# A power-of-two scale's sum over partitions takes its PSUM buffer from another pool, in an attention and hard-swish kernel

## The chip, the cores and the metric

The kernel runs on one core of a Trainium2 chip. The metric is the device time in microseconds (us), as the median of several runs. The engines are named as in the profile: PE (TensorE, matmul), PEld (its weight loads), DVE (VectorE), ACT (ScalarE), POOL (GpSimd) and SP (SyncE, which here issues the DMAs).

## The reference

Attention with a decay over 8 batches of 8 heads, 576 positions and head size 64, and behind it two layers with a hard swish on the 4608 rows of 512:

```python
scores = scale * np.matmul(q, k.transpose(0, 1, 3, 2))
cum = np.cumsum(np.log(np.clip(f, 0.0001, 1.0)), axis=-1)
scores = np.where(causal, -1e9, scores + cum[:, :, :, None] - cum[:, :, None, :])
attn = softmax(scores)
x = np.matmul(attn, v).transpose(0, 2, 1, 3).reshape(B * S, H * D)
h = x @ w_in                        # 512 -> 2048
g = h * np.clip(h + 3.0, 0.0, 6.0) / 6.0
return g @ w_out                    # 2048 -> 512
```

## The kernel before

**Numbers in pairs.** The two layers multiply fp16 pairs: each operand is scaled by a power of two and split into a high and a low half, and three matmuls (high x high, high x low, low x high) stand for one. The power of two of a weight comes from the sum of its squares. For w_out, `w_decode` squares each of 16 chunks on ACT (L257) into columns of `wsum`, `w_sum` adds the columns on DVE (L279, tile wm), and `pow2_scale` adds over the 128 partitions with one matmul against ones (L184, tile pt_w) into a PSUM tile, which four small DVE operations (L187, L189, L193, L196) turn into the scale. Only then can the sixteen chunks be split: `w_split` writes the high half on ACT (L284) and the low half on DVE (L295), 128x512 elements each. `pow2_scale` serves w_in (four scales, columns S1 to S1+3 of the tile SC), w_out (column S2) and the v of each batch (columns SV to SV+7).

**The attention.** The heads are worked through as a list of 68 entries. Entries 0 to 3 take the first 256 positions of two heads each of batch 0, entries 4 to 11 the remaining positions of its 8 heads, and from entry 12 on each entry is one whole head of batches 1 to 7 (entries 12 to 19 are batch 1). For entries up to 11 the row maxima come from matmuls pn (L495) and a DVE reduction (L501); a PE transpose ptm (L510) and DVE (L512, tile mr) turn them into a row that a DMA (L513) puts into TQ, where the scores ps (L559 to L562) need it. From entry 12 on, `rows` makes the scores pn in two halves (L619 and L622, 12 matmuls in all), DVE masks them and takes maxima (L630, L636), ACT takes the exponential (L642) and casts (L656), DVE and POOL subtract for the low half (L659, L665, L670), a transposing DMA (L677) turns both, and 40 matmuls pav (L702 to L707) multiply with v; DVE normalizes (L738 to L740, L746). Three ring buffers hold the halves in front of the DMA. POOL prepares q and k of coming entries (L449 to L469), and `v_split` splits v (L399 on ACT, L400 on DVE).

**The two layers.** `h_unit` makes a tile ph of the first layer (twelve matmuls, L788 to L790, of 128x256 for the first and second part of batch 0 and 128x512 later), read by ACT (L794) and DVE (L797, the last reader of the PSUM tile) and written as a pair (L798, L799). `out_unit` makes a tile po of the second layer (48 matmuls, L835 to L837, 128x512), which ACT scales (L841) and a DMA writes out (L844). For batch 0 there are 16 ph tiles for rows 0 to 255, then po_0 and po_1 of these rows, then 16 ph tiles for rows 256 to 511, then po_2 and po_3.

**PSUM.** Eight banks: `ps_s` (2 tiles of 2 banks: pn and ps), `ps_m` (2 tiles of one bank, tag "mm": ph, po and pt of the weights), `ps_t` (1 tile, tag "tr": ptm, pt of v, and every third ph or po where `mm_tile` is given `three`, which is false for the rows 0 to 255 of batch 0) and `ps_a` (1 tile: pav). A tile that is taken from a pool waits until the tile that had its buffer is read.

**What sets the order.** The code at the end of the kernel writes the work entry by entry: the steps of the attention, `w_step` for one step of the weights' work, and `fill` for as much of the layers as a credit allows. A scheduler then orders each engine's instructions, with that order as priority, the tiles' dependences and the pools' buffers as conditions. In the order that the code is written in, pt_w takes its tile behind all sixteen ph tiles of rows 0 to 255.

Of the kernel before, what the change touches and what calls it, by code (L numbers as in the profile page):

```python
# [20 lines left out]
def kernel(  # L21
# [14 lines left out]
    B = vS.shape[0]  # L36
# [19 lines left out]
    ps_m = ctx.enter_context(tc.tile_pool(name="ps_m", bufs=2, space=bass.MemoryType.PSUM))  # L56
    ps_t = ctx.enter_context(tc.tile_pool(name="ps_t", bufs=1, space=bass.MemoryType.PSUM))
# [21 lines left out]
    )  # L79

    NQK, NL, NST = 3, 2, 3
    W_RATE = (8, 5, 4)
    H_COST = 1.05
    F_RATE = (0.6, 0.45, 1.06)
    PIN = 0
# [67 lines left out]
    SV, IV, UO, UX, A1 = 0, 8, 16, 24, 32  # L153
    S1, I1, S2, I2, S1R, I1R, SW2 = 64, 68, 72, 73, 74, 75, 76
# [24 lines left out]


    def pow2_scale(pm, s_col, i_col, name):
        pool, tag = (ps_t, "tr") if SV < s_col < SV + B else (ps_m, "mm")
        pt = pool.tile([P, 512], F32, tag=tag, name=f"pt_{name}")
        nc.tensor.matmul(pt[:, 0:1], ones, pm, start=True, stop=True)  # L184
        yield
        e = p2.tile([P, 2], F32, tag="ee", name=f"e_{name}")
        nc.vector.tensor_scalar(e[:, 0:1], pt[:, 0:1], 2.0 ** -100, None, op0=ALU.max)  # L187
        ei = e.bitcast(I32)
        nc.vector.tensor_scalar(  # L189
            ei[:, 1:2], ei[:, 0:1], 24, 23, op0=ALU.logical_shift_right, op1=ALU.logical_shift_left  # L190
        )
        si = SC.bitcast(I32)
        nc.vector.tensor_scalar(  # L193
            si[:, s_col:s_col + 1], ei[:, 1:2], -1.0, float(204 << 23), op0=ALU.mult, op1=ALU.add
        )
        nc.vector.tensor_scalar(  # L196
            si[:, i_col:i_col + 1], ei[:, 1:2], 1.0, float(50 << 23), op0=ALU.mult, op1=ALU.add
        )
        yield
# [97 lines left out]
    def w_in_work():  # L297
        first, ahead = W_AHEAD
        for k in range(first):
            w_load(0, k, slots_in)  # L300
        yield
        for k in range(first, ahead):
            w_load(0, k, slots_in)
        for j in range(NG):
            ks = range(j * NCC, (j + 1) * NCC)
            for k in ks:
                if k + ahead < NW:
                    w_load(0, k + ahead, slots_in)
                w_decode(0, k, slots_in)
                yield  # L310
            pm = w_gram(ks) if GRAM[j] else w_sum(ks[0], ks[-1] + 1)
            yield
            yield from pow2_scale(pm, S1 + j, I1 + j, f"w0{j}")
            eye = None
            if PE_LOW[j]:
                eye = p2.tile([P, DM], F32, tag="o", name=f"eye{j}")[:, 0:P]
                nc.vector.tensor_scalar(
                    eye, identf, scol(S1 + j), -1.0, op0=ALU.mult, op1=ALU.mult
                )
            for k in ks:  # L320
                w_split(0, k, scol(S1 + j), eye)
                yield
            w_in_done.append(j)

    def w_out_work():
        n = len(slots_out)
        for k in range(n):
            w_load(1, k, slots_out)
        yield

        for k in range(NW):
            w_decode(1, k, slots_out)
            if k + n < NW:
                w_load(1, k + n, slots_out)
            yield
        for _ in range(W_GAP):
            yield
        yield from pow2_scale(w_sum(NW, 2 * NW), S2, I2, "w1")
        nc.vector.tensor_reduce(scol(S1R), SC[:, S1:S1 + NG], axis=AX.X, op=ALU.min)
        nc.vector.tensor_reduce(scol(I1R), SC[:, I1:I1 + NG], axis=AX.X, op=ALU.max)  # L340
        nc.vector.tensor_scalar(
            SC[:, SW2:SW2 + NG], SC[:, I1:I1 + NG], scol(S1R), scol(S2),
            op0=ALU.mult, op1=ALU.mult,
        )
        for k in range(NW):
            w_split(1, k, scol(SW2 + k // NG))
            yield
# [15 lines left out]
    def v_scale(b):  # L363
        pm = p2.tile([P, 2], F32, tag="pm", name=f"vm{b}")
        for i, t in enumerate(v_parts(b)):
            most = nc.vector.tensor_reduce(
                pm[:, i:i + 1], t.rearrange("p c (h e) -> p (c h) e", e=D + 1)[:, :, 0:D],
                axis=AX.XY, op=ALU.max, apply_absolute_value=True,
            )
            if b:  # L370
                tc.keep_in_program_order(most)
            yield
        nc.vector.tensor_tensor(pm, pm, pm, op=ALU.mult)
        nc.vector.tensor_tensor(pm[:, 0:1], pm[:, 0:1], pm[:, 1:2], op=ALU.max)
        yield from pow2_scale(pm[:, 0:1], SV + b, IV + b, f"v{b}")
# [594 lines left out]
    for i, (kind, n) in enumerate(VH):  # L970
        b, h = divmod(n, H)
        if kind == "A":
            b = h = 0
        wn = W_RATE["ABF".index(kind)]
        rates[0] = F_RATE[0] if kind == "B" else F_RATE[min(b, 2)]
# [101 lines left out]
```

## Time and profile before

| | us |
|---|---|
| median of 3 runs | 1061.22 (1059.41 to 1063.06) |
| profiled execution | 1060.59 |
| its span | 1058.5 |
| PE busy | 1006.1 |
| DVE busy | 714.1 |
| ACT busy | 633.0 |
| POOL busy | 440.0 |

An engine's busy time counts its own instructions, and the engines work beside each other. The mean TensorE clock granted over the span is 0.987 of full speed. In the answers of the trace a row of a timeline has the start in us, the duration, the engine, the line, the operation with its shapes, and in brackets the idle time before it and what ended that; a row of a group has the busy time in us, the mean of one in ns, and the idle time ahead; the rows of stretches are explained where they stand.

### The profile page before, as it was taken

To read this page: it belongs to the slowest core of one execution; us is meant where nothing else is said; L and a number is where in the kernel's file an instruction comes from. 1 tells how busy PE (TensorE), PEld (TensorE's weight loads), DVE (VectorE), ACT (ScalarE), POOL (GpSimd) and SP (SyncE) were. 2 spreads that over 40 slices of the span, in tenths; PEclk is the share of its full clock that TensorE was granted. 3 is DMA by queue.
4 is the path that set the end of the run, shared out by engine and by line. 5 is a ranking of instruction groups with operands and counts; after the bars stand their busy time and mean duration, and the time that the engine had idled before them with its cause. 6 is when DMAs were issued, how large, how long until landed. Compare 5 with 4: busy or idle time off the path is not lost.

```text
span 1058.5 us, 21322 instructions
## 1 busy us (share of the span) xinstructions
PE 1006.1 (95%) x7650; PEld 599.4 (57%) x7650; DVE 714.1 (67%) x1887; ACT 633.0 (60%) x1257; POOL 440.0 (42%) x641
## 2 busy tenths in 40 slices
PE   2799978899999999999999999999999999999998
PEld 1567845675555755555555755555555755444553
DVE  6878799876876678865885678956886677204310
ACT  5798667766864667655764667655765567205312
POOL 9634556525444444454544455544544441000000
PEclk9989989999999999999999999999999999999999
DMA  7875346936765765566565665557565644101001
GB/s 245 271 214 180 98 103 128 209 88 133 154 108 128 129 146 112 90 136 159 109 120 109 133 154 104 107 119 162 109 109 122 118 94 67 21 1 40 1 11 41
DMA packets 253717, 123.83 MB, mean 117 GB/s; under 512 B 225860, under 2 KB 227452, under 8 KB 253612
## 3 DMA queue, kind: packets, MB, share of 16 engines
q1 hardware_dynamic: 253612, 122.47, 53.0%
q8 instruction: 60, 0.98, 0.4%
q14 instruction: 45, 0.37, 0.1%
HBM read 47.93 MB, written 9.73 MB: 54 GB/s over the span
## 4 chain that ended last, share of the span: by engine, by line
PE 80%; DVE 9%; DMA 4%; ACT 4%; issue 2%; SPq 0%; POOL 0%; ACTq 0%; DVEq 0%; POOLq 0%
PE ph L788 10%; PE po L835 10%; PE po L837 10%; PE po L836 10%; PE ph L789 10%; PE ph L790 10%; PE pn L622 3%; PE pn L619 3%; PE pav L706 1%; PE pav L707 1%; PE ph_r L811 1%; PE pav L705 1%; PE ph_r L812 1%; PE ph_r L813 1%; PE po_r L835 1%
## 5 line engine op out<-in xcount | busy, mean ns | idle before, releaser
L642 ACT ACTIVATE pp<-pp,nb 128x192 f32<-128x192 f32 x280 | 138.4, 552 | 133.9 <-DVE nb L636 116.7
L788 PE MATMUL ph<-xT,w 128*128 128x512 f16 (+1 forms) x576 | 197.0, 358 | 3.6 <-ACT o L841 2.3
L659 DVE TENSOR_TENSOR ring<-pp,ring 128x128 f16<-128x128 f32 (+2 forms) x216 | 141.4, 668 | 83.5 <-ACT ring L656 77.8
L789 PE MATMUL ph<-xT,w 128*128 128x512 f16 (+1 forms) x576 | 196.3, 357 | 0.0
L790 PE MATMUL ph<-xT,w 128*128 128x512 f16 (+1 forms) x576 | 196.0, 357 | 0.0
L836 PE MATMUL po<-w,gT 128*128 128x512 f16 x512 | 192.8, 382 | 3.2 <-DVE w L295 3.2
L464 POOL TENSOR_TENSOR T<-ST,TQ 64x288 fp32r<-64x288 f32 (+2 forms) x136 | 112.4, 828 | 200.4 <-PE pn L622 152.1
L835 PE MATMUL po<-w,gT 128*128 128x512 f16 x512 | 191.0, 383 | 4.5 <-ACT w L284 3.9
L837 PE MATMUL po<-w,gT 128*128 128x512 f16 x512 | 192.3, 382 | 0.0
L630 DVE CUSTOM_DVE_ANT_0 pp<-pn,W 128x192 f32<-128x192 f32 x280 | 123.5, 484 | 33.0 <-PE pn L622 22.9
L794 ACT ACTIVATE r<-ph,bias_r,SC 128x512 f32<-128x512 f32 (+1 forms) x144 | 103.2, 726 | 64.9 <-PE ph L790 61.6
L797 DVE SCALAR_TENSOR_TENSOR r<-r,ph 128x512 f32<-128x512 f32 (+1 forms) x144 | 89.0, 621 | 75.8 <-ACT r L794 75.3
L619 PE MATMUL pn<-TK,TQ 68*128 68x192 f32 x336 | 125.9, 388 | 5.2 <-issue 4.9
L469 POOL TENSOR_TENSOR T<-ST,T 64x288 fp32r<-64x288 f32 (+1 forms) x136 | 126.0, 945 | 11.5 <-ACT T L462 6.9
L622 PE MATMUL pn<-T,T 128*128 128x192 f32 x336 | 115.8, 370 | 0.0
L656 ACT CAST ring<-pp 128x192 f16<-128x192 f32 x280 | 114.5, 450 | 0.2
L799 DVE TENSOR_TENSOR gT<-r,gT 128x512 f16<-128x512 f32 (+1 forms) x144 | 102.7, 718 | 15.5 <-ACT gT L798 13.8
L798 ACT CAST gT<-r 128x512 f16<-128x512 f32 (+1 forms) x144 | 80.9, 567 | 33.2 <-DVE r L797 32.3
L665 POOL TENSOR_TENSOR ring<-pp,ring 128x128 f16<-128x128 f32 x96 | 56.2, 585 | 104.2 <-ACT ring L656 84.3
L837 PEld LDWEIGHTS <-gT 128*128 128x128 f16 x560 | 54.7, 98 | 69.5 <-issue 9.8
L836 PEld LDWEIGHTS <-gT 128*128 128x128 f16 x560 | 54.9, 98 | 61.6 <-issue 6.6
L790 PEld LDWEIGHTS <-w 128*128 128x128 f16 x576 | 56.4, 98 | 56.6 <-issue 6.6
(159 smaller groups left out, 2036.4 us busy)
## 6 DMA issues: line engine op xcount, KB each, us to landing
ST<-in_qk_dram SPq DMA_DIRECT2D x64, 288.0 KB
ring<-in_w_out_dram SPq DMA_DIRECT2D x16, 512.0 KB
out_dram<-o SPq DMA_DIRECT2D x32, 256.0 KB
T<-TQ SPq DMA_DIRECT2D x56, 144.0 KB
vst<-in_vS_dram SPq DMA_DIRECT2D x7, 1040.0 KB
ring<-in_w_in_dram SPq DMA_DIRECT2D x9, 512.0 KB
w<-in_w_in_dram SPq DMA_DIRECT2D x7, 512.0 KB
vst<-in_vS_dram SPq DMA_DIRECT2D x14, 130.0 KB
```

The costliest lines, as they stand in the source:

```text
L469: nc.gpsimd.tensor_tensor(T1[j][0:D, a:e], s[D:, a:e], T1[j][D:, a:e].bitcast(F32), op=ALU.subtract)
L619: nc.tensor.matmul(dst, TQ[i][0:D + 4, qs], TK[i][0:D + 4, a:e], start=True, stop=False)
L622: nc.tensor.matmul(dst, T7[j][:, qs], T1[j][:, a:e], start=False, stop=True)
L630: nc.vector.tensor_tensor_reduce(pp[:r, w:w + kw], pn[:r, o:o + kw], W[:r, 4 * P + r - kw:4 * P + r], 1.0, -3.0e38, ALU.add, ALU.max, accu ...
L642: nc.scalar.activation(x_, x_, AF.Exp, bias=nb[:r, e0 + x:e0 + x + 1], scale=0.125)
L659: eng.tensor_tensor(hl[:r, a:a + c * P], pp[:r, at[c] + 64:at[c] + kw], hl[:r, h0[c] + 64:h0[c] + kw], op=ALU.subtract,)
L788: nc.tensor.matmul(ph, w1[0][:, cc, fs_], xh, start=(cc == 0), stop=False)
L789: nc.tensor.matmul(ph, w1[0][:, cc, fs_], xl, start=False, stop=False)
L790: nc.tensor.matmul(ph, w1[1][:, cc, fs_], xh, start=False, stop=(cc == NCC - 1))
L835: nc.tensor.matmul(po, g[:, 0, fc, ts_], w2[:, fc, 0, :], start=(fc == 0), stop=False)
L836: nc.tensor.matmul(po, g[:, 0, fc, ts_], w2[:, fc, 1, :], start=False, stop=False)
L837: nc.tensor.matmul(po, g[:, 1, fc, ts_], w2[:, fc, 0, :], start=False, stop=(fc == NFC - 1))
```

## The change

`pow2_scale` chooses the pool of its one PSUM tile. Before, only the scales of v for batches 1 to 7 used ps_t; the scale of w_out now does so too. The scales of w_in stay in ps_m. (The other line of the diff changes only spaces.)

```diff
-    W_RATE = (8, 5, 4)
+    W_RATE = (8,5,4)
...
     def pow2_scale(pm, s_col, i_col, name):
-        pool, tag = (ps_t, "tr") if SV < s_col < SV + B else (ps_m, "mm")
+        pool, tag = (ps_t, "tr") if SV < s_col < SV + B or s_col == S2 else (ps_m, "mm")
         pt = pool.tile([P, 512], F32, tag=tag, name=f"pt_{name}")
```

Since the pools' buffers are conditions of the scheduler, it gives another order. On PE, at the place where entry 11 (tile pn_0_1435) begins, the new order against the old:

```order
 L495 MATMUL pn_0_1435<-TK_98,TQ_95 128x512
 L495 MATMUL pn_0_1435<-TK_98,TQ_95 128x384
+L184 MATMUL pt_w_1354<-wm_1352,ones 128x1
 L713 MATMUL pav<-v_111,pf_1320 128x96 x2
 L788 LDWEIGHTS w_113
```

and further on, within the first half of entry 12 (tile pn_0_1671), where po_0 (tile po_0_1398, the second layer's first) now begins:

```order
 L622 MATMUL pn_0_1671<-T_99,T_101 128x256
 L619 MATMUL pn_0_1671<-TK_96,TQ_93 64x64
-L184 MATMUL pt_w_1354<-wm_1352,ones 128x1
 L622 MATMUL pn_0_1671<-T_99,T_101 64x64
+L835 LDWEIGHTS gT
+L835 MATMUL po_0_1398<-w_115,gT 128x512
```

The matmul pt_w has moved ahead by the ph tiles 10 to 14, the scores of entries 10 and 11 and most of a half of entry 12. The transpose ptm of entry 10, which uses the same buffer of ps_t, has moved from ahead of ph_9 to behind ph_10. The matmuls of po_0 and po_1 now stand in one block with the rest of entries 11 and 12, ahead of entry 13; before they were spread between entries 13 and 18. The 16 ph tiles of rows 256 to 511 now stand between the pn of entries 13 to 18; before they came behind entry 18.

On DVE, at the same first place (w_115 is the tile of w_out's halves, SC the tile of the scales, e_w_1356 the scale's exponent, r_10 and r_11 the tiles behind ph_10 and ph_11):

```order
+L193 TENSOR_SCALAR SC<-e_w_1356 128x1
+L196 TENSOR_SCALAR SC<-e_w_1356 128x1
+L512 TENSOR_SCALAR mr_1413<-ptm_1411 3x128
+L341 TENSOR_SCALAR SC<-SC 128x4
+L386 TENSOR_TENSOR SC<-SC 128x1
 L797 SCALAR_TENSOR_TENSOR r_10_0_1111<-r_10_0_1111,ph_10_0_1098 128x256
+L388 COPY SC<-SC 64x1
+L295 SCALAR_TENSOR_TENSOR w_115<-w_115,SC 128x512
 L501 ISA junk_2_1451,MC_107<-pn_1_1448,W 64x576
 L501 ISA MC_107 64x1
 L799 TENSOR_TENSOR gT<-r_10_0_1111,gT 128x256
```

The scale's operations and the first split L295 now stand among the work of ph_10; before, the first split stood behind both halves' L630 of entry 12. Six splits now stand ahead of entry 12's first row operation, and all sixteen ahead of entry 13's; before they were spread up to entry 18.

On DVE again, in the stretch where entries 16 and 17 are now worked on (tiles pn and pp of entry 16 end in 2232 to 2289, those of entry 17 in 2392 and 2401), after the change:

```order
L797 SCALAR_TENSOR_TENSOR r_9_256_2270<-r_9_256_2270,ph_9_256_2257 128x256
L636 TENSOR_SCALAR nb_2231<-MF_108 128x2
L799 TENSOR_TENSOR gT<-r_8_256_2176,gT 128x256
L659 TENSOR_TENSOR ring_125<-pp_0_2241,ring_125 128x128
L659 TENSOR_TENSOR ring_125<-pp_0_2241,ring_125 128x512
L665 TENSOR_TENSOR ring_125<-pp_0_2241,ring_125 128x2x64
L670 TENSOR_TENSOR ring_125<-pp_0_2241,ring_125 64x64
L797 SCALAR_TENSOR_TENSOR r_10_256_2308<-r_10_256_2308,ph_10_256_2295 128x256
L799 TENSOR_TENSOR gT<-r_9_256_2270,gT 128x256
L630 ISA pp_0_2401,MF_109<-pn_0_2392,W 128x192
```

Here each entry's row operations stand in turn with those of the ph tiles of rows 256 to 511; before, splits of w_out stood between the row operations of these entries.

## The prediction

> **What bounds the kernel now.** I read the page's busy times first, then the busy time by stretch, then PE's waits in the one stretch where PE idles, then the timelines of DVE and PE there.
>
> ```profile
> span 1058.5 us, 21322 instructions
> PE 1006.1 (95%) x7650; PEld 599.4 (57%) x7650; DVE 714.1 (67%) x1887; ACT 633.0 (60%) x1257; POOL 440.0 (42%) x641
> ```
>
> PE is busy 95% of the span, so the time is PE's work plus the places where PE waits. The stretches show where those lie (columns: stretch, length, busy us of PE, PEld, DVE, ACT and POOL, granted clock, DMA share, GB/s):
>
> ```profile
> 100.00:125.00 25.00, 25.00 (x214) 21.86 (x214) 16.90 (x48) 17.19 (x36) 8.79 (x15) 1.00 0.41 123
> 125.00:150.00 25.00, 18.23 (x137) 14.44 (x135) 24.26 (x69) 16.03 (x32) 20.18 (x25) 0.93 0.26 68
> 150.00:175.00 25.00, 22.21 (x175) 14.27 (x176) 23.77 (x67) 18.77 (x40) 14.39 (x19) 0.87 0.76 149
> 175.00:200.00 25.00, 18.17 (x158) 10.95 (x156) 23.28 (x63) 18.38 (x37) 17.65 (x21) 0.88 0.76 173
> 250.00:400.00 150.00, 149.54 (x1262) 88.14 (x1259) 111.16 (x292) 96.32 (x193) 72.46 (x110) 1.00 0.66 133
> 430.00:665.00 235.00, 234.43 (x1889) 134.55 (x1887) 173.90 (x451) 148.32 (x295) 111.71 (x168) 1.00 0.61 124
> ```
>
> Between 125 and 200 us PE idles 75 - 58.61 = 16.4 us, and there DVE is busy 71.3 of 75 us. In the 25 us just ahead DVE has 8 us free and PE none; from 250 us on PE is full again and DVE is not. So one stretch is DVE's, and work that DVE did earlier would shorten it. The idle time also costs clock:
>
> ```profile
> 140.00:150.00 10.00, 3.23 (x15) 1.21 (x13) 9.94 (x21) 6.61 (x15) 6.35 (x7) 0.82 0.17 46
> 150.00:160.00 10.00, 9.04 (x58) 5.90 (x59) 8.85 (x29) 7.38 (x15) 3.52 (x5) 0.67 0.85 157
> 180.00:190.00 10.00, 7.83 (x55) 3.73 (x53) 9.96 (x28) 7.86 (x17) 5.14 (x7) 0.83 0.74 145
> 190.00:200.00 10.00, 7.39 (x54) 4.71 (x53) 8.46 (x25) 7.19 (x16) 8.02 (x10) 0.88 0.93 231
> 200.00:210.00 10.00, 9.98 (x133) 8.90 (x131) 7.60 (x26) 8.88 (x23) 2.98 (x4) 0.95 1.06 189
> ```
>
> Busy time times missing clock is 0.6 + 3.0 + 1.3 + 0.9 + 0.5 = 6.3 us. The pot that this stretch holds is 16.4 + 6.3 = 22.7 us.
>
> Who PE waits for there (us in total, times, longest):
>
> ```profile
> PE pn L619 <- issue: 4.9, 2, 3.2
> PE po L835 <- ACT w L284: 3.9, 2, 3.5
> PE po L836 <- DVE w L295: 3.2, 3, 1.7
> PE ph L788 <- ACT o L841: 2.3, 1, 2.3
> ```
>
> L284 and L295 split w_out into high and low halves, and the second layer's po consumes them in order. They cannot start before the scale of w_out is known, and that scale hangs on one PSUM buffer:
>
> ```profile
> 110.75 0.15 DVE L279 TENSOR_REDUCE wm<-wsum 128x1 f32<-128x16 f32 x1
> 114.89 0.67 PE L495 MATMUL pn<-TK,TQ 66*128 66x512 f32 x2
> 133.72 0.36 PE L184 MATMUL pt_w<-wm,ones 128*128 128x1 f32 x2
> 141.36 0.75 DVE L295 SCALAR_TENSOR_TENSOR w<-w,SC 128x512 f16<-128x512 f32 x1
> 193.87 0.74 DVE L295 SCALAR_TENSOR_TENSOR w<-w,SC 128x512 f16<-128x512 f32 x1
> ```
>
> The per-partition sums wm are there at 110.9. The sum over partitions, pt_w, runs only at 133.7: the code takes its tile behind the sixteen ph tiles of the first 256 rows, from the same two buffers of ps_m, so it waits for all but the last of them to be read. Then the sixteen splits take from 141.4 to 194.6, scattered between the attention's work on a full DVE.
>
> **The change, part by part.** One [P,512] tile moves from the pool that the ph tiles rotate through to ps_t; no instruction is added or removed. What it moves:
>
> *The scale.* In the new order pt_w stands right behind the pn matmuls of entry 11, which before ran at 114.9. By then wm has been ready for 4 us, so PE does not wait. That is 18 us earlier (133.7 - 115.4). The four small DVE operations of pow2_scale follow, so the first split can stand near 119 instead of 141.4.
>
> *The splits.* Before the first row operation of entry 12 DVE now has six of the sixteen splits. What it has room for there:
>
> ```profile
> 115.00:134.00 19.00, 19.00 (x162) 16.88 (x162) 14.22 (x29) 12.25 (x23) 12.14 (x17) 1.00 0.46 131
> L295 DVE SCALAR_TENSOR_TENSOR w<-w,SC 128x512 f16<-128x512 f32 x16 | 13.5, 843 | 0.4 <-ACT w L284 0.3
> ```
>
> One split occupies DVE about 0.77 us (843 ns, of which the next instruction overlaps some 0.07, as ends and starts in the timeline do). 14.2 + 6 x 0.77 = 18.8 of 19 us: it just fits, and what hides it is DVE's free time of 4.8 us. If the ph tiles' L797 comes late behind a split, PE waits for a PSUM buffer. I give this 1.5 us of new PE idle time (0 to 4.6, the whole of the six splits).
>
> *The transpose that now waits.* ptm of entry 10 uses the only buffer of ps_t, so it must wait until L187 has read pt_w. It moves behind ph_10, to about 117. Queued behind it on PE is the next ph; its reader L512 stands on DVE behind L196; and the row it sends by DMA is needed by entry 10's scores, some 4 us later. For entry 11 that distance was
>
> ```profile
> 122.38 0.28 DVE L512 TENSOR_SCALAR mr<-ptm 3x128 fp32r<-3x128 f32 x1 [0.66 <-PE ptm L510]
> 126.84 0.40 PE L559 MATMUL ps<-TQ,TK 97*128 97x320 f32 x1
> ```
>
> 4.5 us, without a wait on PE. I cost it at nothing beyond the 1.5 us; its cover is about 4 us, and if that were gone it would cost 1 to 2 us once.
>
> *The second layer's first two tiles.* Before, the 96 matmuls of po_0 and po_1 were spread in pieces over entries 13 to 18. Now they stand in front of entry 13, so from about 134 on PE has
>
> ```profile
> 142.60 0.38 PE L836 MATMUL po<-w,gT 128*128 128x512 f16 x1
> 142.81 0.38 PE L837 MATMUL po<-w,gT 128*128 128x512 f16 x1
> ```
>
> 96 x 0.215 = 20.7 us of them, with some 4 us of entries 11 and 12 between. DVE has in this stage ten splits (7.7) and entry 12 (6.5, below, its share of the split of v included): 14.2 us, and some more for the next entries' share of v, against 25. PE is ahead of the splits only at the end of po_0; I take 1.5 us of idle time (0 to 5).
>
> Their results' two output DMAs also move up in SP's queue, ahead of the decay and rest loads of entries 15 and 16. SP waits there for L841 until about 160. The loads of entries 13 and 14 stand ahead of them, so a whole entry of work covers the delay: nothing, or 2 us if that cover is too short.
>
> *What is late next.* The attention of entries 13 to 18, which before ran while PE waited for splits, now runs behind po, together with the 16 ph tiles of 256 rows. Between the end of po_1 and the start of po_2 stand 5.5 entries and 16 tiles. The prices:
>
> ```profile
> 151.00:190.40 39.40, 33.35 (x287) 20.80 (x288) 37.79 (x99) 30.36 (x62) 24.42 (x30) 0.89 0.72 144
> 151.00:190.40 39.40, 11.99 (x14) 0.89 0.72 144
> L799 DVE TENSOR_TENSOR gT<-r,gT 128x256 f16<-128x256 f32 x26 | 12.3, 486 | 2.6 <-ACT gT L798 2.4
> L797 DVE SCALAR_TENSOR_TENSOR r<-r,ph 128x256 f32<-128x256 f32 x24 | 9.8, 413 | 4.2 <-ACT r L794 4.1
> 190.42 0.34 PE L619 MATMUL pn<-TK,TQ 68*128 68x192 f32 x1
> 191.35 0.61 PE L835 MATMUL po<-w,gT 128*128 128x512 f16 x2
> 174.89 0.19 PE L702 MATMUL pav<-v,pT 128*128 128x65 f16 x1
> 174.92 0.20 PE L703 MATMUL pav<-v,pT 128*128 128x64 f16 x1
> 112.08 0.27 PE L788 MATMUL ph<-xT,w 128*128 128x256 f16 x1
> 112.19 0.27 PE L789 MATMUL ph<-xT,w 128*128 128x256 f16 x1
> ```
>
> The first two rows are all of DVE and L295 alone, over four entries (pn of entry 14 to pn of entry 18): (37.79 - 11.99) / 4 = 6.45 us of DVE for one entry. A tile costs DVE 413 + 486 ns less two overlaps, 0.76 us. So DVE needs 5.5 x 6.45 + 16 x 0.76 = 47.7 us. PE needs 1.8 us for one entry's pn (two halves of 0.93 and a little less), 40 x 0.031 = 1.25 for its pav, and 12 x 0.11 = 1.32 for a tile: 5.5 x 3.05 + 16 x 1.32 = 37.9 us. A ph tile frees its PSUM buffer only when L797 has read it, and three such buffers rotate, so PE cannot run away from DVE: this stage gives 9.8 us of idle time back (0 to 16, below).
>
> *The clock.* In the row of 150 to 160 the clock is 0.67 after idle times of 3.5 and 3.2 us. The new stage has its idle time in pieces of some 1 us; I keep 1 us of loss (0 to 6.3). [...]
>
> *The sum.* Returned: 1.5 + 1.5 + 9.8 + 1 = 13.8 of 22.7 us. Gain 8.9 us. Past this stage nothing else changes: both orders are alike again on PE from the tile ph_10 of batch 1 on, and PE is full in the rows above from 250 us on, so time won is kept. The profiled execution took 1060.59 us (span 1058.5 and 2.1 around it), 0.6 below the median of 1061.22. 1060.6 - 8.9 = 1051.7, on the median 1052.3; I say 1052.
>
> **Rivals.**
>
> *The whole pot but little returned.* DVE's operations vary in length here: L295 is 843 ns on average and 0.74 us in the row of 193.87, 12% less. With POOL less in the way, DVE's 47.7 us would shrink by as much, to 42, and by a fifth to PE's 37.9; then nothing comes back in this stage and the gain is 8.9 + 9.8 = 18.7: 1042.5. For it: a little later PE was full with entries and tiles mixed, though with fewer entries,
>
> ```profile
> 200.00:250.00 50.00, 49.98 (x460) 36.03 (x458) 36.14 (x115) 32.79 (x74) 17.52 (x24) 0.99 0.60 122
> ```
>
> and DVE had 14 us free. Against: POOL, with 24.4 us of work over four entries, 6.1 for each, stays beside DVE.
>
> *Entries run at their old pace whatever DVE has to do.* Four entries took 39.4 us, 9.85 each, and if ring buffers and the transposing DMAs set that pace, 5.5 entries take 54.2, which is 6.5 more than I count. Gain 2.4: about 1059, no change. Against: DVE was 96% busy in those 39.4 us.
>
> *Slower: the cold clock comes to stay.* The new stage makes PE wait for a PSUM buffer every tile. If these short gaps lower the clock, PE's 37.9 us grow. Down to a clock of 0.79 DVE's 47.7 us hide it; at 0.67, as between 150 and 160, the stage takes 56.6 and the whole gain is gone; at 0.6 it takes 63.2, which is 15.5 more than counted: slower by 6.6, 1068. It decides from a mean clock of 0.67 down. For it: 0.67 to 0.88 stand in the rows above where PE is paced by others. Against: between 170 and 180 PE is busy only 7.95 us of 10, and the trace has
>
> ```profile
> 170.00:180.00 10.00, 7.95 (x86) 5.60 (x85) 9.81 (x26) 7.44 (x17) 7.06 (x9) 1.00 0.51 112
> ```
>
> a clock of 1.00. [...]
>
> *The change does not do what it says.* If ps_t were held until after 133, nothing would move: 1061. The new order has the matmul at the place of 115, so this is nearly out.
>
> **How the numbers follow.** Forecast 0.55, little returned 0.17, old pace 0.16, cold clock 0.10, no effect 0.02. A measurement of this kernel can tell about 0.3%, 3.2 us, from no change: faster means under 1058, slower over 1064.4. The forecast's own bounds (run-up 0 to 4.6, second layer 0 to 5, the clock 0 to 6.3) reach from 1048 to 1059, so a small part of it is no change, and the old pace is no change or a small gain. Faster 0.73, same 0.16, slower 0.11. The range reaches down to the little-returned case and up past the old pace: 1042 to 1062, leaving out half of the former and the cold clock.
>
> **What would show it.** Right: pt_w near 115, the first split near 119 and the sixteenth before 150; po_0 and po_1 in one block from about 134 to 160 with under 4 us of PE idle time; then some 48 us with DVE full, PE idle about 10 and waiting for L797 or row operations; PE full from about 210. Wrong: PE full behind po (the gain is larger), a clock under 0.7 there, or long waits of ps L559 for the mr DMA or of po for L295 between 119 and 160.

## The result, and the profile after

The changed kernel takes 1056.5 us (median of 8 runs, 1053.2 to 1058.5) beside 1062.4 us for the kernel before on the same chip (8 runs, 1059.4 to 1065.3): ratio 0.9942, 95% interval 0.9926 to 0.9957. A second comparison, experiment e1 below, gave 0.9923 (0.9906 to 0.9940). So the change saves about 6 to 8 us; the forecast was 9.

The spans of the two profiled executions, 1058.5 and 1056.6 us, differ by less than that. To see why, I looked for a piece of work on PE ahead of which all stands alike in both orders (the first pn of entry 10, one entry ahead of the place of pt_w) and one behind which all is alike again (ACT's copy of po_0 of batch 1). Timeline rows of PE and of ACT, and the one stretch between these two rows (columns as in the prediction), first before:

```profile
105.50 0.65 PE L495 MATMUL pn<-TK,TQ 66*128 66x512 f32 x2
316.01 0.69 ACT L841 ACTIVATE o<-po,SC 128x512 f32<-128x512 f32 x1
105.50:316.01 210.51, 193.63 (x1584) 129.22 (x1581) 172.80 (x483) 146.91 (x304) 110.70 (x148) 0.96 0.60 129
```

and after:

```profile
108.07 0.65 PE L495 MATMUL pn<-TK,TQ 66*128 66x512 f32 x2
313.63 0.69 ACT L841 ACTIVATE o<-po,SC 128x512 f32<-128x512 f32 x1
108.07:313.63 205.56, 193.11 (x1584) 130.97 (x1581) 170.85 (x483) 147.94 (x303) 108.83 (x148) 0.96 0.61 132
```

Both stretches hold the same work: 1584 matmuls and 483 DVE operations in each. I call this the stage. It shrank from 210.5 to 205.6 us. What lies ahead of it took 2.6 us longer in this profiled execution, in work that stands alike in both orders; in the other profiles of this study the same row stands between 105.39 and 107.68. What lies behind the stage takes 742 to 743 us in both (1058.5 - 316.0 and 1056.6 - 313.6). With a second profile of each kernel (stages of 211.2 and 203.8) the change is worth 210.9 - 204.7 = 6.2 us in the stage, which is what the timings say. A span alone would have told a third of it.

Now the same stretches as in the prediction, after the change:

```profile
100.00:125.00 25.00, 25.00 (x215) 21.84 (x214) 20.28 (x60) 18.25 (x39) 8.24 (x14) 1.00 0.38 106
125.00:150.00 25.00, 25.00 (x163) 16.78 (x162) 22.33 (x58) 20.15 (x39) 15.40 (x18) 1.00 0.35 99
150.00:175.00 25.00, 20.70 (x164) 14.94 (x163) 17.65 (x49) 13.05 (x26) 12.63 (x15) 0.92 0.45 106
175.00:200.00 25.00, 21.74 (x221) 18.60 (x221) 24.12 (x77) 22.05 (x52) 13.75 (x17) 0.84 0.91 178
225.00:250.00 25.00, 22.58 (x217) 13.66 (x215) 21.55 (x72) 16.11 (x35) 14.72 (x24) 1.00 0.75 158
250.00:275.00 25.00, 22.53 (x140) 12.91 (x139) 22.44 (x54) 21.23 (x42) 15.53 (x23) 0.93 0.73 148
```

PE's hole of 125 to 150 is gone; two smaller ones stand between 150 and 200, and two new ones behind 225, where before PE was full. DVE is full only from 175 to 200. What moved (timeline rows of PE, DVE and ACT):

```profile
117.86 0.28 PE L184 MATMUL pt_w<-wm,ones 128*128 128x1 f32 x2
121.83 0.75 DVE L295 SCALAR_TENSOR_TENSOR w<-w,SC 128x512 f16<-128x512 f32 x1 [0.34 <-ACT w L284]
136.62 0.40 PE L835 MATMUL po<-w,gT 128*128 128x512 f16 x1
156.08 0.75 DVE L295 SCALAR_TENSOR_TENSOR w<-w,SC 128x512 f16<-128x512 f32 x1 [0.80 <-ACT w L284]
159.16 1.27 ACT L841 ACTIVATE o<-po,SC 128x512 f32<-128x512 f32 x2 [3.12 <-PE po L837]
```

With the 2.6 us by which this execution started late taken off, pt_w (115.3), the first split (119.3) and the begin of the po block (134.0) stand where the forecast put them. The block ends 3 us before the forecast's 160, and the sixteenth split, at 153.5, is later than the 150 forecast and paced by ACT's half of it. All that PE waited for between 100 and 260 us:

```profile
PE ph L788 <- DMA xT<-xhl: 6.8, 2, 4.3
PE pav L702 <- DMA pT<-ring: 3.5, 2, 3.3
PE pn L619 <- issue: 2.2, 1, 2.2
```

Not one of these names DVE, which the prediction had made the pace there. The longest, 4.3 us, has a chain that can be read row by row (timelines of DVE, ACT, SP's DMA queue and PE; entry 11's pav ends at 160.8):

```profile
161.51 0.22 DVE L734 TENSOR_SCALAR rs<-pav,SC 128x3 f32<-128x3 f32 x1
165.74 0.34 DVE L740 TENSOR_TENSOR xf<-pav,rs 128x192 f32<-128x192 f32 x1
167.13 0.50 ACT L745 CAST xhl<-xf 128x384 f16<-128x384 f32 x1
167.66 1.05 DVE L746 TENSOR_TENSOR xhl<-xf,xhl 128x384 f16<-128x384 f32 x1 [0.96 <-ACT xhl L745]
169.11 1.21 SPq L759 DMA_TRANSPOSE xT<-xhl  x1
170.38 1.25 SPq L763 DMA_TRANSPOSE xT<-xhl  x1
172.87 0.37 PE L788 MATMUL ph<-xT,w 128*128 128x256 f16 x1 [4.30 <-DMA xT<-xhl]
```

In the changed order entry 11's pav matmuls stand singly between those of the po block and end some 23 us later than before; its rows xT are then late for the last quarter of the first ph tiles of rows 256 to 511. And around the two longest gaps the clock is low:

```profile
170.00:180.00 10.00, 7.13 (x37) 5.70 (x37) 9.28 (x27) 7.40 (x19) 6.67 (x8) 0.56 0.69 146
180.00:190.00 10.00, 10.00 (x114) 8.70 (x113) 9.77 (x33) 9.10 (x22) 6.01 (x8) 0.93 0.75 144
190.00:200.00 10.00, 6.74 (x85) 5.80 (x84) 10.00 (x34) 7.95 (x19) 5.38 (x7) 0.92 1.17 225
```

The gap of 2.2 us at 230 left it at 1.00 (the row from 225 above). So two readings stood against each other. Theory A, the prediction's: DVE's work sets the pace, whatever PE's last wait is called. Theory B: it is what the waits say, the late transposes of xT and pT, and the cold clock behind them.

### The profile page after: what moved, and what is told of

Same layout as the page of the kernel before. It is cut to its first block, busy times and chain, and to the rows that moved or that the text cites. A ratio compares the mean times of both kernels' runs of the same rounds, so it can differ in the third digit from the quotient of the medians.

```text
span 1056.6 us, 21330 instructions
## 1 busy us (share of the span) xinstructions
PE 1006.6 (95%) x7650; PEld 601.7 (57%) x7650; DVE 712.9 (67%) x1887; ACT 634.9 (60%) x1257; POOL 437.8 (41%) x641
## 4 chain that ended last, share of the span: by engine, by line
PE 80%; DVE 6%; DMA 6%; ACT 4%; issue 2%; POOL 1%; SPq 0%; ACTq 0%; DVEq 0%
PE po L835 10%; PE po L837 10%; PE po L836 10%; PE ph L788 9%; PE ph L789 9%; PE ph L790 9%; PE pn L619 4%; PE pn L622 4%; PE pav L713 2%; DMA w<-in_w_in_dram 1%; PE ph_r L811 1%; PE ph_r L812 1%; PE ph_r L813 1%; PE pav L706 1%; PE po_r L835 1%
## 5 line engine op out<-in xcount | busy, mean ns | idle before, releaser
L788 PE MATMUL ph<-xT,w 128*128 128x512 f16 (+1 forms) x576 | 198.9, 361 | 7.6 <-DMA xT<-xhl 6.8
L659 DVE TENSOR_TENSOR ring<-pp,ring 128x128 f16<-128x128 f32 (+2 forms) x216 | 138.9, 657 | 83.6 <-ACT ring L656 82.9
L630 DVE CUSTOM_DVE_ANT_0 pp<-pn,W 128x192 f32<-128x192 f32 x280 | 123.6, 484 | 32.0 <-PE pn L622 20.2
L794 ACT ACTIVATE r<-ph,bias_r,SC 128x512 f32<-128x512 f32 (+1 forms) x144 | 103.7, 728 | 63.3 <-PE ph L790 61.0
L797 DVE SCALAR_TENSOR_TENSOR r<-r,ph 128x512 f32<-128x512 f32 (+1 forms) x144 | 89.1, 621 | 73.4 <-ACT r L794 72.7
L469 POOL TENSOR_TENSOR T<-ST,T 64x288 fp32r<-64x288 f32 (+1 forms) x136 | 125.2, 939 | 11.6 <-ACT T L462 6.9
L619 PE MATMUL pn<-TK,TQ 68*128 68x192 f32 x336 | 125.5, 387 | 2.2 <-issue 2.2
L799 DVE TENSOR_TENSOR gT<-r,gT 128x512 f16<-128x512 f32 (+1 forms) x144 | 106.9, 744 | 13.7 <-ACT gT L798 11.8
L665 POOL TENSOR_TENSOR ring<-pp,ring 128x128 f16<-128x128 f32 x96 | 55.6, 580 | 108.3 <-ACT ring L656 92.1
```

Of the source, the lines that this page charges most:

```text
L469: nc.gpsimd.tensor_tensor(T1[j][0:D, a:e], s[D:, a:e], T1[j][D:, a:e].bitcast(F32), op=ALU.subtract)
L619: nc.tensor.matmul(dst, TQ[i][0:D + 4, qs], TK[i][0:D + 4, a:e], start=True, stop=False)
L630: nc.vector.tensor_tensor_reduce(pp[:r, w:w + kw], pn[:r, o:o + kw], W[:r, 4 * P + r - kw:4 * P + r], 1.0, -3.0e38, ALU.add, ALU.max, accu ...
L659: eng.tensor_tensor(hl[:r, a:a + c * P], pp[:r, at[c] + 64:at[c] + kw], hl[:r, h0[c] + 64:h0[c] + kw], op=ALU.subtract,)
L788: nc.tensor.matmul(ph, w1[0][:, cc, fs_], xh, start=(cc == 0), stop=False)
```

## The experiments

All edits are made in the changed kernel, except in e5, which is the kernel before. A ratio is to the kernel before on the same chip and has an interval of 0.0012 to 0.0020 to each side, 1.3 to 2.1 us; the stage is measured between the two rows named above, and profiles of one kernel differ in it by 0.7 (before) and 1.8 us (after). Each edit also makes the scheduler order anew, so a variant differs from the changed kernel in more than its edit: matmul by matmul, PE's sequence in the stage agrees with the changed kernel's to 98% in e2, 92% in e3 and some 75% in e4, e6 and e10.

| run | median us | ratio (95% interval) | stage us | PE idle in it | DVE busy in it |
|---|---|---|---|---|---|
| before | 1062.4 | | 210.5 | 16.9 | 172.8 |
| e5, before again | 1061.4 (one run) | | 211.2 | 17.9 | 173.7 |
| changed | 1056.5 | 0.9942 (0.9926 to 0.9957) | 205.6 | 12.5 | 170.9 |
| e1, changed again | 1053.7 | 0.9923 (0.9906 to 0.9940) | 203.8 | 12.2 | 171.6 |
| e2, less DVE | 1050.3 | 0.9901 (0.9883 to 0.9920) | 199.9 | 9.7 | 163.8 |
| e3, xT first | 1055.3 | 0.9936 (0.9921 to 0.9951) | 204.2 | 11.6 | 170.0 |
| e4, entry 11 first | 1052.3 | 0.9910 (0.9892 to 0.9929) | 202.6 | 10.8 | 167.2 |
| e6, more DVE | 1067.2 | 1.0054 (1.0042 to 1.0066) | 217.1 | 18.7 | 181.1 |
| e7, e2 and e4 | 1051.3 | 0.9919 (0.9899 to 0.9939) | 200.5 | 10.3 | 163.0 |
| e8, POOL and e4 | 1052.5 | 0.9918 (0.9902 to 0.9934) | 202.6 | 10.3 | 167.2 |
| e9, other pool | 1058.6 | 0.9980 (0.9967 to 0.9993) | 210.4 | 14.4 | 176.6 |
| e10, gap filled | 1054.2 | 0.9939 (0.9927 to 0.9951) | 203.8 | 10.9 | 172.5 |
| e11, rows in the block | 1056.0 | 0.9952 (0.9939 to 0.9966) | 206.1 | 13.9 | 173.2 |
| e12, the same otherwise | 1051.5 | 0.9913 (0.9899 to 0.9927) | 201.5 | 11.7 | 169.4 |

Each stage's row of the trace gives its last three columns: length, length less PE's busy time, DVE's busy time. In e3 four matmuls more than in the others stand inside the stage, in e10 two more beside the 32 that were added. e1 to e4 ran on one chip, so the time of e1, 1053.7, is the one to set beside e2, e3 and e4.

**e1, e5: both kernels again.**

> The changed kernel unaltered, as the yardstick for the runs beside it. Both theories expect what was measured before: 1056.5 us, ratio to the kernel before about 0.994. A second profile of it should show the same two waits of PE behind po_1 if they belong to the order of the work (ph L788 for xT near 173, about 4 us; pav L702 for pT near 198, about 3 us); if they were chance, they are gone or elsewhere.

> The kernel before unaltered, for a second profile. If the waits of PE between 125 and 200 belong to the order of the work, they come again (po L835 for ACT L284 3.9 us in all, po L836 for DVE L295 3.2, pn L619 4.9, ph L788 for L841 2.3), and PE's busy time from 0 to 100 tells whether the 1.5 us by which the changed kernel's profiles lag there (68.8 against 70.3) is chance.

The waits came again to 0.2 us in the changed kernel (4.3 and 3.1 us), and in kind before (po for L284 3.5 us in all, for L295 6.1, pn L619 3.2, ph for L841 2.3). They belong to the order. PE's busy time from 0 to 100 was 68.8 us in e5 too, so it does not explain the late start; the first of the two rows stands at 105.73 there, at 107.68 in e1 and at 105.39 to 106.86 in the other variants of the changed kernel, whose start is the same work. I take the late start for chance.

**e2, e6: DVE's work taken away and doubled.** In e2

```diff
-        nc.vector.tensor_tensor(gT[:, 1, fc, c0:c1], r, gT[:, 0, fc, c0:c1], op=ALU.subtract)
+        if not (b == 0 and c0 > 0):
+            nc.vector.tensor_tensor(gT[:, 1, fc, c0:c1], r, gT[:, 0, fc, c0:c1], op=ALU.subtract)
...
-            nc.tensor.matmul(po, g[:, 1, fc, ts_], w2[:, fc, 0, :], start=False, stop=(fc == NFC - 1))
+            lo = 0 if name == "0" and s > 1 else 1
+            nc.tensor.matmul(po, g[:, lo, fc, ts_], w2[:, fc, 0, :], start=False, stop=(fc == NFC - 1))
```

and in e6 the same operation stands twice for `b == 0 and c0 > 0`. e2 (and e7, which contains it) leaves a part of the product out and is of use for its time only.

> Leaves out the low halves of the hidden layer (L799) for rows 256 to 511 of batch 0; the second layer's third matmul reads the high half in their place, so PE's work is the same. That takes 16 x 0.486 less overlaps = 6.6 us from DVE between 160 and 210. Theory A (the prediction's: DVE's work bounds that stage and gives 9.8 us of idle time back): the stage shrinks by about 6 us, 1050.5. Theory B (a chain of latencies does it: entry 11's pav matmuls are late, so the transposed rows xT come late, PE waits 4.3 us once and runs cold for 7 us behind it): the wait for xT stays at about 4 us and the time falls by under 2 us, 1055 to 1056.

> The changed kernel with L799 issued twice for the 16 tiles of rows 256 to 511 of batch 0: 16 x 0.486 less overlaps = 7 us more for DVE between 160 and 230, the mirror image of leaving it out. Theory A (DVE's work bounds the stage): 6 us slower than the changed kernel, about 1060, and PE waits for L797 and row operations. Theory B (the late xT and pT transposes bound it): under 2 us slower, 1054 to 1056.

The stages of the two, in which the DVE operations left out and added show in the counts (468 and 499 against 483):

```profile
106.22:306.16 199.94, 190.27 (x1584) 129.13 (x1581) 163.84 (x468) 147.23 (x305) 105.94 (x149) 0.97 0.63 135
```

```profile
105.53:322.63 217.10, 198.45 (x1584) 132.77 (x1581) 181.10 (x499) 148.50 (x304) 110.72 (x148) 0.94 0.57 125
```

Against the mean of the changed kernel's two profiles, 204.7 us with 171.2 of DVE, 7.4 us less of DVE took 4.7 off the stage, and 9.9 more put 12.4 on it. In e6 PE's waits name DVE at once, beside the same 4.3 us for xT:

```profile
PE ph L788 <- DMA xT<-xhl: 8.2, 3, 4.3
PE ph L788 <- DVE r L797: 5.6, 2, 3.2
```

Theory A predicted 6 and 6, theory B under 2 both times. By the timings e2 saved 3.4 us beside e1, about half of theory A's 6; that it came out at the 1050.5 of the expectation is luck, since that counted from 1056.5. The wait for xT stood at 4.3 us in both runs, so it did not set the time. In e6 more came on than the DVE work added: PE idled 6.3 us more and was busy 6.1 us more, at a mean clock of 0.94. Its order on PE is another from 185 us on, so how much of the 12.4 us is DVE's work alone is not shown; e2 is the cleaner of the two.

The trace of the changed kernel also has DVE in front of both waits that name a DMA. From the end of entry 11's pav at 160.9 to the end of xhl at 168.7 DVE was busy 6.8 of 7.8 us: the division L740 came only at 165.7, behind splits of v (L400) and another entry's row operations (L630, L636). And in the 12.4 us up to the end of the wait for pT, from 186.0 to 198.4, DVE was busy without a break.

**e3: the transpose that is needed first.**

```diff
-        if rest is not None:
-            nc.sync.dma_start_transpose(xT[2]...)
         nc.sync.dma_start_transpose(xT[b % 2]...)
+        if rest is not None:
+            nc.sync.dma_start_transpose(xT[2]...)
```

> In x_move the transpose that the next ph tiles need (L763) is issued ahead of the one for the rest rows (L759), which are needed much later. Theory B: xT lands about 1.2 us sooner, the wait at 173 falls from 4.3 to about 3.1 and the time by 1 to 2.5 us, 1054 to 1055.5. Theory A: DVE sets the pace, so the time stays at 1056.5 within 1.

The wait fell from 4.3 to 3.4 us, and neither the time (1055.3, 1.6 us over e1) nor the stage (204.2) is shorter than the changed kernel's beyond the spread: as theory A has it, though 1055.3 by itself would lie in theory B's range.

**e4: entry 11 first.**

```diff
-            av(*prev)
+            with tc.high_priority(offset=200) if prev[0] == NPAIR + H - 1 else nullcontext():
+                av(*prev)
```

> Entry 11's pav matmuls and the divisions behind them get a priority 200 higher, so that they stand ahead of most of po_0 and po_1 instead of singly between their matmuls; nothing else is edited. Theory B: xT is there before 165, the 4.3 us wait and the cold clock behind it (about 4 us) go, 1049 to 1053. Theory A: DVE's sum in the stage is the same, so PE waits elsewhere instead: 1055.5 to 1057.5.

The wait for xT is gone, and what PE waits for between 160 and 210 us has new names and comes in small pieces:

```profile
PE pav L702 <- DMA pT<-ring: 3.3, 4, 1.5
PE ph L788 <- DVE r L797: 2.6, 4, 1.1
PE pn L619 <- PE ph L790: 0.4, 1, 0.4
```

The stage is 2.1 us shorter, and the time 1.4 us under e1's, between the two theories; the timings (0.9910 beside 0.9942 and 0.9923) do not decide how much is real. PE idles 10.8 us in the stage instead of 12.3: when the one long wait goes, most of it is paid elsewhere.

**e7, e8: combined.** e7 is e2 and e4 together; e8 is e4 with every second of the 16 subtractions on POOL (`eng = nc.gpsimd if b == 0 and c0 > 0 and fc % 2 else nc.vector`).

> Both cures at once: L799 left out for rows 256 to 511 of batch 0 (the second layer reads the high half there instead) and entry 11's pav given its priority. Alone they took 3.3 and 1.4 us off. Theory A (DVE alone bounds; the priority only moved the wait): about the same as without L799 alone, 1049 to 1051. Theory C (DVE's work and the late xT are two limits that stand beside each other, each hiding the other's cure): the sum is more than 3.3 + 1.4, 1043 to 1047. Theory B alone: 1049.

> A version meant to be of use, complete: entry 11's pav with its priority, and every second L799 of those 16 tiles on POOL, 8 x 0.43 = 3.4 us off DVE and, at the 0.84 to 0.95 us that POOL takes for a 64x288 row, 8 us more on POOL. Theory A: 2 to 3 us under the priority alone, 1049 to 1050. Rival: POOL's operations there are slower beside DVE's or its row work comes late, and the time stays at 1052 or goes up.

e7 (stage 200.5) is no shorter than e2 alone (199.9), so theory C, two limits side by side, falls. e8 has e4's stage to 0.1 us and its time too, as the rival of its expectation had it: half of the subtractions on POOL brought nothing, and in DVE's busy time they took nothing off (167.2 in both). The eight subtractions are gone from DVE (475 operations in the stage for 483; L799 there took 26.0 us in e4, 22.7 in e8), but the same 50 operations L659 took 30.5 us in place of 27.0. A sum of fixed prices for DVE, as the prediction made it, does not hold here.

**e9: another pool.**

```diff
-        pool, tag = (ps_t, "tr") if SV < s_col < SV + B or s_col == S2 else (ps_m, "mm")
-        pt = pool.tile([P, 512], F32, tag=tag, name=f"pt_{name}")
+        pool, tag = (ps_t, "tr") if SV < s_col < SV + B else (ps_s, "S") if s_col == S2 else (ps_m, "mm")
+        pt = pool.tile([P, 1024 if pool is ps_s else 512], F32, tag=tag, name=f"pt_{name}")
```

The tile is then one of the two that the scores pn and ps share.

> The sum over partitions of w_out's scale takes its tile from ps_s, the pool of the scores, in place of ps_t; the rest is as in the changed kernel. If the gain is that the scale is known some 18 us sooner, any pool with a buffer free near 115 does: 1053.5 to 1056.5, the same as the changed kernel. If what counts is that ps_t in particular makes ptm of entry 10 wait (and with that shifts the entries), it is nearer to 1061.

Counted from the first pn of entry 10, pt_w runs 1.5 us earlier than in the changed kernel (8.3 us for 9.8) and the last split 3.8 us earlier (44.2 for 48.0); and yet nearly all of the gain is gone (0.9980, stage 210.4). In this order the po block begins before entry 12's first half is through: its last small pn matmul stands behind some 90 of the 96 po matmuls. The first row operation of entry 12 on DVE, and DVE's work under the block:

```profile
155.31 0.36 DVE L630 CUSTOM_DVE_ANT_0 pp<-pn,W 128x192 f32<-128x192 f32 x1 [3.58 <-PE pn L622]
136.60:160.00 23.40, 23.40 (x127) 13.11 (x126) 13.30 (x38) 11.94 (x21) 4.94 (x6) 1.00 0.14 42
```

In the changed kernel they are

```profile
137.06 0.34 DVE L630 CUSTOM_DVE_ANT_0 pp<-pn,W 128x192 f32<-128x192 f32 x1
136.60:160.00 23.40, 23.40 (x123) 12.63 (x122) 15.99 (x43) 14.29 (x28) 8.97 (x11) 1.00 0.30 68
```

So an early scale is not enough. Whether it pays hangs on what else the scheduler then puts behind the block. DVE's busy time in the stage is higher too, 176.6 for 170.9 us, for nearly the same operations (487 and 483); the same 50 operations L659 took 33.6 us for 28.3.

**e10: the gap filled.** 32 matmuls with a result that is thrown away, ahead of those tiles:

```diff
+        if b == 0 and c0 and fc == 0:
+            for k in range(32):
+              with tc.high_priority(offset=60):
+                nc.tensor.matmul(ph, w1[0][:, 0, fs_], w1[1][:, 0, 0:nw], start=True, stop=True)
```

> The changed kernel with 32 matmuls more, 128x256, whose result is thrown away, in PE's order between pn of entry 13 and the first ph of rows 256 to 511, where PE waits 4.3 us for xT: 32 x 0.107 = 3.4 us, so that 0.9 us of the gap is left; the first ph needs xT as before. Theory D (a gap is paid twice: PE's clock stood at 0.5 and 0.67 for 10 us behind it, 4.3 us of work lost): the clock there is 1.00 and the time falls by 3 to 4 us, 1050 to 1053. Theory A (DVE paces PE behind the gap anyway): the clock is 1.00 but PE waits for DVE's L797 or row operations instead, and the time stays within 1 us of 1054 to 1056.

They stand some 6 us ahead of the wait, behind the pn of entry 13, and push what follows into the gap. The clock holds, and the wait for xT has gone; PE waits for DVE instead (L794 and L803 are L788 and L797, six lines further down; two stretches, then PE's waits from 165 to 185):

```profile
160.00:170.00 10.00, 10.00 (x116) 8.84 (x115) 7.99 (x31) 5.81 (x14) 6.23 (x8) 1.00 0.28 66
170.00:180.00 10.00, 7.98 (x97) 7.00 (x96) 8.77 (x24) 9.53 (x22) 9.23 (x13) 1.00 0.65 143
```

```profile
PE ph L794 <- DVE r L803: 2.5, 1, 2.5
PE pav L702 <- DMA pT<-ring: 0.8, 1, 0.8
```

The stage is 203.8 us and the time 1054.2, the same as the changed kernel. PE's own matmuls took 189.3 us of the stage (192.9 less 3.7 for the added ones), 3.1 less than in the mean of the changed kernel's profiles; but PE idled or ran the added matmuls for 14.5 us instead of 12.3. Of its waits up to 260, 7.0 us name DVE. So theory D is not borne out: most of what the clock gave back went into other waits. The order on PE is another as well, so that this is one order's answer.

**e11, e12: rows for DVE under the block.** DVE is busy only 16.0 of the 23.4 us of the po block in the changed kernel (22.2 before). Lower priority for the layers while the entries around it are issued brings entries 13 and 14 into the block:

```diff
-            with tc.high_priority(offset=-LOW_M):
+            low = 400 if prev and 11 <= prev[0] + 1 <= 14 else 0
+            with tc.high_priority(offset=-low):
```

(e12; in e11 it is 200 and from entry 10.)

> The changed kernel with the tiles of the two layers 200 lower in priority while entries 10 to 14 are issued, so that the pn of entries 13 and 14 and the pav of entries 11 to 13 stand between the matmuls of po_0 and po_1 instead of behind them; the rest of the program is as it was. Theory E (the block of 96 po matmuls gives DVE nothing to do: it idled 6.9 us between 136.6 and 159.5, and was the pace from 160 on): DVE works through the block, and the time falls by 3 to 6 us from the changed kernel's 1053.7 to 1056.5, to 1048 to 1053. Rival (what paces the stage is the way of one entry, row operations, transposing DMA, pav, division, however early it starts): 1054 to 1056.5.

> The same idea with 400 from entry 11 on: pn of entry 13 stands after half of the po matmuls and all of entry 14's after three quarters, and the rows 256 to 511 begin two entries earlier than in the run beside it. Theory E: 1048 to 1053 as well, the better one being the one in which DVE idles less under the block. Rival: 1054 to 1056.5.

The same stretch in e11 and in e12:

```profile
136.60:160.00 23.40, 21.14 (x134) 12.63 (x133) 22.52 (x66) 16.92 (x35) 13.19 (x16) 1.00 0.39 89
```

```profile
136.60:160.00 23.40, 23.40 (x131) 13.76 (x129) 21.21 (x62) 14.90 (x29) 13.08 (x16) 1.00 0.35 76
```

In both DVE works through the block. In e12 the time is 1051.5, and its four runs (1050.1 to 1052.6) lie below thirteen of the changed kernel's fourteen; in e11 it is 1056.0, no gain. In e11 PE already waits in the block (2.3 us idle, in part for splits L295 that came later behind the entries' rows) and po_1 ends 10 us later. So theory E is half borne out: filling DVE there can pay, and what the fill displaces decides. With e4, e12 is the best complete kernel of the study; the two cannot be told apart.

## Why the prediction was right, and where it was wrong

The direction holds, and so does the mechanism up to the po block; behind it DVE bounds the stage as forecast, but not by the wait that was named. The gain is two thirds of the forecast: 6.2 us in the stage for 8.9. Step by step:

- **The scale and the splits.** Right: 18 us earlier, and PE without a wait from 100 to 168.6 us. The run-up's 1.5 us and the second layer's 1.5 us were nothing. ptm of entry 10 behind pt_w cost nothing, as said: its row leaves DVE at 120.6 and ps needs it at 124.5, without a wait. SP's two output DMAs held up nothing that PE waited for.
- **The stage behind the block.** Forecast: 47.7 us with DVE full and 9.8 idle on PE. From the end of po_1 to po_2 (159.5 to 210.35) it took 50.8 us with 7.6 idle, and DVE was busy 44.6. The size is near, and e2 shows that it hangs on DVE's work, with e6 and e10 beside it in orders of their own; but DVE was not full all through (3.7 of its 6.3 idle us stand behind 200), and PE's last wait was for a transpose, not for L797. The step "PE waiting through PSUM buffers" is wrong as a description of this order; it came true where DVE had more to do (e6) or the long wait for xT was gone (e4, e10).
- **"PE is full again from about 210".** Wrong: two waits of 2.2 and 2.5 us stand at 230 and 255. They make up for the 3 us that the run-up and the second layer did not cost and the 2.2 that the stage was under its 9.8. The idle time in all is 12.3 us of 17.4 (12.8 of 16.4 forecast), right by errors that cancel, which is luck.
- **The clock.** This term failed: 1 us put down, of 6.3; that 1 us was an estimate, which no run shows. The mean clock of the stage is 0.96 and 0.97 after, 0.96 before: at 193 us busy, that is 6 to 8 us each time, as far as two digits tell. Taken in stretches of 1 us, the granted clock is 0.50 in 17.1 us of the stage in both profiles before, and in 17.1 and 13.7 us after: next to nothing came back. The premise was idle time in pieces of some 1 us; it came in pieces of 4.3, 3.3, 2.2 and 2.5. e4, where the pieces between 160 and 210 us are 1.5 at most, has a clock of 1.00 there, so the premise was the error and not the price.
- **The sum.** Idle time gave 17.4 - 12.3 = 5.1 us (3.6 forecast) and PE's busy time, clock included, 193.5 - 192.4 = 1.1 (5.3 forecast). But in e10 the two did not simply add: with the clock back, PE waited for DVE. A sum of PE's idle and cold time then counts as two terms what one slower engine sets.
- **The rivals.** "Cold clock" told that at a clock of 0.79 or more DVE would hide it; in 160 to 210 the mean was 0.86, and e10 speaks for it being hidden. "Old pace": 9.85 us an entry would have made 54.2 us of this stage, 47.7 were forecast, 50.8 came, half way between. That ring buffers and transposing DMAs set this pace is not shown; e2 speaks for DVE. "Little returned" needed a lighter DVE, and e2 shows about that: 7.4 us less of DVE, 4.7 us less of stage. Its premise, that DVE's operations are longer beside POOL's, shows in the profile before: of the sixteen L295 the seven with POOL busy for over 80% of their time took 0.97 us on average, the six with under 20% took 0.74.

Still open: why e9's order and e11's lose and e12's wins, beyond the single rows shown; I have no order in which DVE is fed through the block without moving the splits. Nor does any run take the early scale apart from the order that comes with it, so how much of the gain is due to each is not shown. Why the same DVE operations take longer in one order than in another is open too.

## What to carry to other kernels

When one engine paces a stage, the wait that the profile names on another engine is only the last of several. Take it away before believing it (e4 and e10 did, for 2 us or less), and change the pacing engine's work in both directions to see the slope, measured between two rows that all variants share and not in spans. Where a scheduler decides, a buffer's pool sets the order of the whole stage: the same operation as early or earlier was worth 6 us from one pool and 2 from another.

## What the runs showed of the hardware

In the changed kernel the ten us that hold the end of the gap of 4.3 us have a mean clock of 0.56, the ten behind 0.93 (rows from 170 and 180 above); in stretches of 1 us it is 0.50 from about 171 to 181 and 1.00 from 182 to 198. Around a gap of 2.4 us in e4 it is 0.66 and 0.83:

```profile
223.74 0.22 PE L702 MATMUL pav<-v,pT 128*128 128x65 f16 x1 [2.39 <-DVE xf L740]
220.00:230.00 10.00, 6.76 (x66) 5.80 (x65) 9.97 (x30) 5.49 (x13) 9.34 (x13) 0.66 0.77 183
230.00:240.00 10.00, 10.00 (x40) 4.19 (x39) 7.56 (x31) 7.13 (x17) 4.44 (x7) 0.83 1.06 178
```

The gap of 2.5 us in e10 ends at 181.3, in a row with 0.83:

```profile
180.00:190.00 10.00, 8.67 (x90) 7.23 (x90) 9.11 (x33) 6.84 (x17) 1.92 (x4) 0.83 0.74 155
```

Gaps of this length do not always cost clock. The changed kernel's gap of 2.47 us, which ends at 255.2, stands with 0.83 from 250 to 260; in e1 the same gap (2.48 us) left that stretch at 1.00 (the clock of 210 to 260 is 1.00 there, with 4.8 us of idle time), and the gap of 2.17 us at 230 left it at 1.00 in both.

In the kernel before a gap of 2.28 us, which ends at 198.0, stands with 0.88 from 190 to 200 (0.50 from 198 on), and even waits of 1.65 us, at 169 and 179, stand ahead of a stretch at 0.50 (181 to 183). Waits of up to 1.5 us, nine of them within 50 us in e4, left it at 1.00, where the changed kernel's longer ones brought the same stretch to 0.86 (e4, then the changed kernel):

```profile
160.00:210.00 50.00, 43.68 (x456) 34.42 (x455) 45.71 (x141) 40.30 (x92) 32.86 (x43) 1.00 0.90 174
```

```profile
160.00:210.00 50.00, 42.44 (x439) 36.64 (x438) 44.21 (x139) 38.75 (x89) 30.90 (x38) 0.86 0.72 152
```

With matmuls of no use ahead of the gap the clock was 1.00 from 160 to 180 (e10). One and the same DVE operation varies in length: L665 on 128x128 elements took 0.27 to 1.00 us within the changed kernel's profile. And the first 105 us vary by 2.7 us from run to run (105.39 to 108.07 for the same row), more than most edits here are worth.
